# Attention in native float32 with exponentials transposed by TensorE, and half of a weight product beside batch 0

## The chip, the cores and the metric

The kernel runs on one core of a Trainium2 chip. The metric is the device time of one execution in microseconds (us), a median of several runs. Engines are named as the profile names them: PE is TensorE (PEld its weight loads), DVE is VectorE, ACT is ScalarE, POOL is GpSimd, SP is SyncE, which issues the DMAs of this kernel.

## The reference

Four batches, eight heads, 576 positions, head size 64; then two gated products over the 2304 x 512 result. Weights come as float64.

```python
scores = scale * q @ k.T + bias          # scale 1/8, bias -slope[h] * |i - j|
mask = (rel >= 0) & (rel < 128)          # rel = i - j: a causal window of 128
attn = exp(scores - max); attn /= attn.sum(-1) + 1e-9
x = attn @ v                             # to 2304 x 512, heads side by side
x = (x @ w_a) * (x @ w_b) @ w_out        # 512 -> 1536 -> 512
a, b = x @ w1, x @ w2                    # 512 -> 1024
out = (a * b @ w3) @ w_out2              # 1024 -> 1024 -> 512
```

## The kernel before

**Precision.** TensorE takes float32 operands in a reduced form (fp32r), so each float32 value is split in a high and a low part and a product is made of three matmuls: low x high, high x low, high x high. This holds for the scores, for every gated product and for w3 by w_out2.

**Attention.** A unit is one batch and two heads (`units`, 16 of them, batch by batch). Its five query blocks of 128 positions (the last has 64) are done in three runs, `RUNS = ((0, 1), (2, 3), (4,))`. `prep` transposes the unit's q and k on TensorE (ten tiles of 128 x 128) and splits them in a high and a low part. For each run, `scores` makes the three products for each block and head; `step_exps` adds the bias and takes the row's extreme on VectorE (L338), then the exponential and its sum on ScalarE (L344). One run later `norms` makes the reciprocals and `probs` multiplies the exponentials by them, written as two float16 parts (L372, L376, L378), which a DMA transpose issued by SP (L383) turns round. `LAG` runs after the scores, `pv` multiplies by v: v is split in three bfloat16 parts by GpSimd, and five of the part products are made, the two heads in the two halves of the array's columns; v is the stationary operand. `pv_out` splits the result in x_hi and x_lo. `keep_warm` issues matmuls on filler data in the first units. A PSUM pool of three tiles (`ps_t`) holds the transposed q and k and the products with v.

**Beside attention.** `Filler` issues steps of the first group of gated products (group 0: `g1`, L546, and `g2_two`, L572) in tiles of 256 tokens, once the group's six weight tiles are ready and the tokens' attention is finished, worth `FILL` us of TensorE per run. `Stages` works off a list of weight loads and conversions from float64 bits (`convert`: two passes on ScalarE, three on VectorE, one on GpSimd, then the split); `PACE` says how many turns it takes per run, in batch 0 and after it.

**After attention.** The ten steps of group 0 that are left, then groups 1 to 9 of the gated products, tile by tile, all on TensorE at three products each. Beside groups 1 to 4, `w34_parts` makes the product w3 by w_out2, which the last groups use as one weight: two halves of w3's columns, eight row blocks each. A block is four transposes (L454), an eviction and a split, twelve matmuls of 512 columns (L462), an eviction (L464) and a store to DRAM; the two halves are added when they are loaded again.

**Order.** Instructions are ordered by the framework from a simulated schedule, starting from the program's order; each engine then works through its own queue in order.

Of the kernel before, what the change touches and what calls it, by code (L numbers as in the profile page):

```python
# [8 lines left out]
F32 = mybir.dt.float32  # L9
# [25 lines left out]
LAG = 3  # L35
FILL = 2.4
PACE = (0.5, 1.0)
TURN = 400
WARM_UNITS, WARM = 3, 2
# [3 lines left out]
def attention_moe_moe(ctx, tc, q, k, v, w_a, w_b, w_o, w_1, w_2, w_3, w_o2, out):  # L43
# [10 lines left out]
    PSC = 2.0 ** 15  # L54
# [42 lines left out]
    def convert(raw, hi=None, lo=None, use=()):  # L97
# [26 lines left out]

        def s3():
            nc.gpsimd.tensor_tensor(out=ai, in0=ai, in1=es[0], op=ALU.add)  # L126
# [54 lines left out]
    sm_p = asb.enter_context(tc.tile_pool(name="sm_p", bufs=2, side="right"))  # L181
    ps_s = asb.enter_context(tc.tile_pool(name="ps_s", bufs=3, space=PSUM))
# [5 lines left out]
    v_raws = [raw_p.tile([P, NB, P], F32, name=f"v_raw{i}") for i in range(3)]  # L188

    def consts():  # L190
# [30 lines left out]
        for t in [t for ts in raws for t in ts] + v_raws:  # L221
            nc.vector.memset(t[:, NB - 1, :], 0.0)
# [7 lines left out]
    def load_unit(u, which=(0, 1, 2)):  # L230
        b, hp = units[u]
        for x in which:
            s = (q, k, v)[x][b, 2 * hp:2 * hp + 2]
            t = raw_of(u)[x] if x < 2 else v_raws[u % 3]
            for j in range(2):
                nc.sync.dma_start(
                    out=t[:, 0:NB - 1, j * D:(j + 1) * D],
                    in_=s[j, 0:(NB - 1) * P, :].rearrange("(c p) d -> p c d", p=P),
                )
            if x:  # L240
                nc.sync.dma_start(
                    out=t[0:LAST, NB - 1, :].rearrange("p (j d) -> p j d", j=2),
# [4 lines left out]
            for j in range(2):  # L247
                o = slice(j * D, (j + 1) * D)
                nc.sync.dma_start(out=t[o, NB - 1, o], in_=s[j, (NB - 1) * P:S, :])
# [4 lines left out]
    qk, vS = {}, {}  # L254

    def prep(u):


        def part(n):
# [3 lines left out]
            def trans():  # L263
                if n == 0:
                    qk[u] = [tr_p.tile([P, 2 * NB * P], F32R, name=f"qk{x}") for x in "hl"]
# [12 lines left out]
        def v_parts():  # L278

            vr = v_raws[u % 3]  # L280
            r1 = tr_p.tile([P, NB, P], F32, name="v1")
            v2 = tr_p.tile([P, NB, P], BF16, name="v2")
            upper = [t.bitcast(BF16).rearrange("p c (f t) -> p c f t", t=2)[:, :, :, 1] for t in (vr, r1)]
            vS[u] = upper + [v2]
            sub(nc.gpsimd, r1, vr, upper[0])
            sub(nc.gpsimd, v2, r1, upper[1])

        return [part(n) for n in range(len(parts))] + [(v_parts, None)]
# [10 lines left out]
    def scores(run):  # L299
# [4 lines left out]
        for u, i in run:  # L304
            hi, lo = qk[u]
# [23 lines left out]
    def step_exps(u, i):  # L329
# [4 lines left out]
        pe = d["pe"] = sm_p.tile([P, 2, 2 * P], F32, name="pe", bufs=5)  # L334
# [13 lines left out]

    def keep_warm(cnt, x):
# [5 lines left out]
    def norms(run):  # L355
        st = live.pop(run)
        nc.vector.tensor_scalar(
            out=st[:, 2], in0=st[:, 1], scalar1=1.0e-9, scalar2=1.0 / PSC, op0=ALU.add, op1=ALU.mult
        )
        nc.vector.reciprocal(out=st[:, 3], in_=st[:, 2])  # L360

    def probs(u, i):
        m, n, nb, nj = window(i)
        d = live[u, i]
        pe, st = d["pe"], d["st"][:, 3]
        pp = sm_p.tile([P, 2 * 2 * 2 * P], F16, name="pp", bufs=5)[:, 0:2 * nj * n].rearrange(
            "p (a b c) -> p a b c", a=nj, b=2
        )

        for j in range(nj):  # L370
            if i == 0:
                nc.vector.tensor_scalar(  # L372
                    out=pp[:, j, 0, :], in0=pe[:, j, :n], scalar1=st[:, j:j + 1], scalar2=None, op0=ALU.mult
                )
            else:
                nc.scalar.activation(pp[:, j, 0, :], pe[:, j, :n], ACTF.Copy, scale=st[:, j:j + 1])  # L376
        for j in range(nj):
            nc.vector.scalar_tensor_tensor(  # L378
                out=pp[:, j, 1, :], in0=pe[:, j, :n], scalar=st[:, j:j + 1], in1=pp[:, j, 0, :],
                op0=ALU.mult, op1=ALU.subtract,  # L380
            )
        t = sm_p.tile([P, 8 * P], F16, name="pt", bufs=6)[:, 0:2 * nj * n]
        nc.sync.dma_start_transpose(  # L383
            out=t.rearrange("p (g m) -> p g m", m=P), in_=pp.rearrange("p a b c -> p (a b c)")
        )

        order = "p (a b c m) -> p a b c m" if nj == 2 else "p (b c a m) -> p a b c m"
        d["pt"] = t, t.rearrange(order, a=2, b=2, c=nb)
# [4 lines left out]
    def pv(run):  # L393
# [4 lines left out]
        for u, i in run:  # L398
            vs = vS[u]
            m, n, nb, nj = window(i)  # L400
            t, pt = live.pop((u, i))["pt"]
            terms = [
                (max(i - 1, 0) + g, g, hl, z)
                for g in range(nb) for hl, z in ((0, 2), (1, 1), (1, 0), (0, 1), (0, 0))
            ]
            for x, (kb, g, hl, z) in enumerate(terms):
                for j in range(2):
                    c = slice(j * D, (j + 1) * D)
                    nc.tensor.matmul(  # L409
                        ps[c, at:at + m], vs[z][:, kb, c], pt[:, j, hl, g, :],  # L410
                        start=(x == 0), stop=(x == len(terms) - 1),
                    )
            at += m
            if u < WARM_UNITS and m == P:
                keep_warm(WARM, t[:, 0:4 * P])

    def pv_out(run):
# [5 lines left out]
        nc.scalar.activation(x_hi[:, hp, o], ps, ACTF.Copy, scale=1.0 / PSC)  # L423
        nc.vector.scalar_tensor_tensor(
            out=x_lo[:, hp, o], in0=ps, scalar=1.0 / PSC, in1=f32(x_hi[:, hp, o]),
            op0=ALU.mult, op1=ALU.subtract,
        )
# [7 lines left out]
    def mm_tile(n):  # L435
        ps = pools["mm"]
        turn[0] += 1
        return ps[turn[0] % len(ps)].tile([P, n], F32, name="mm")

# [212 lines left out]
    def attention_ops():  # L652

        late = []
        for n in range(NR + LAG):
# [29 lines left out]
            if k == RU - 1 and u + 1 < NU:  # L685
                ops.append(trans[RU][0])
# [27 lines left out]
    pools.update(conv=conv_a, raws=1, cas=2)  # L714
# [11 lines left out]
    for f, g in prep(0):  # L726
        f()
        if g:
            g()
    load_unit(1, (0, 1))  # L730
    side.parts += weight_parts(0)
    fl = Filler()
    warm = sm_p.tile([P, 8 * P], F16, name="pt", bufs=6)[:, 0:2 * P]
    nc.vector.memset(warm, 0.0)
    keep_warm(10, warm)
# [34 lines left out]
    side.parts += w34_parts(late, range(2))  # L770
# [27 lines left out]
```

## Time and profile before

| | |
|---|---|
| median of three runs | 998.87 us (995.44 to 999.41) |
| profiled execution | 995.97 us |
| its span, first to last instruction | 994.2 us |
| TensorE busy | 953.7 us (96%) |
| VectorE busy | 533.0 us (54%) |
| ScalarE busy | 430.4 us (43%) |
| GpSimd busy | 399.5 us (40%) |
| DMA | 85.21 MB, mean 86 GB/s |

The busy shares are means over two stages that differ. A busy TensorE is not one at its peak: matmuls overlap, and each is counted to its modelled end. The price of one among many is read from the distance of starts.

### The profile page before, as it was taken

The page shows a single profiled execution, that of the slowest core. Times are in us where ns is not written, and L with a number is a line of the kernel's source. Part 1 is how long each engine was busy: PE and PEld are TensorE (multiplying, and loading weights), DVE is VectorE, ACT ScalarE, POOL GpSimd, SP SyncE. Part 2 cuts the span into 40 slices and gives each one's busy share as a digit, 9 for nine tenths or more (in the row PEclk, how much of TensorE's full clock was granted, in tenths as well). Part 3 has the DMA queues.
Part 4 walks back from the last instruction along what each step waited for, and adds up shares of the span by engine and source line. Part 5 has one row for each costly group of instructions (what it writes and reads, how often), then busy time and mean ns, then how long its engine had stood idle before and what let it go on. Part 6 is the DMA issues. An engine that isn't in the chain of part 4 may idle for free.

```text
span 994.2 us, 16251 instructions
## 1 busy us (share of the span) xinstructions
PE 953.7 (96%) x6162; PEld 802.6 (81%) x6162; DVE 533.0 (54%) x1188; ACT 430.4 (43%) x1003; POOL 399.5 (40%) x329
## 2 busy tenths in 40 slices
PE   8889898888999999999999999999999999999998
PEld 6558787777988788888888888888888888888886
DVE  5979877775689734566474463442442442422222
ACT  5768867775554434434443342343421321311110
POOL 4344122221688423545362362584741631611111
PEclk9968999998999999999999999999999999999999
DMA  5797786764433222323341240120120120000012
GB/s 131 163 185 154 140 140 134 141 127 85 134 121 106 85 96 84 108 75 106 97 126 59 69 139 22 43 85 1 42 85 1 51 78 1 22 1 1 26 65 101
DMA packets 160079, 85.21 MB, mean 86 GB/s; under 512 B 128001, under 2 KB 148993, under 8 KB 160001
## 3 DMA queue, kind: packets, MB, share of 16 engines
q1 hardware_dynamic: 160000, 84.18, 34.1%
q8 instruction: 48, 0.79, 0.3%
q14 instruction: 31, 0.25, 0.1%
HBM read 58.20 MB, written 8.91 MB: 68 GB/s over the span
## 4 chain that ended last, share of the span: by engine, by line
PE 79%; DMA 7%; DVE 6%; ACT 3%; issue 3%; POOL 1%; SPq 1%; POOLq 0%; ACTq 0%; DVEq 0%
PE mm L546 44%; PE mm L583 11%; PE mm L598 10%; PE mm L462 4%; DMA pt<-pp 4%; PE s L312 3%; PE tr L409 3%; PE tr L269 2%; DVE pp L378 1%; PE mm L572 1%; DVE ca L121 1%; DMA raw<-in_moe_w_a 1%; DVE ca L117 1%; POOL ca L126 1%; PE mm L454 1%
## 5 line engine op out<-in xcount | busy, mean ns | idle before, releaser
L72 POOL TENSOR_TENSOR gl<-g,gh 128x512 fp32r<-128x512 f32 (+1 forms) x108 | 123.9, 1148 | 312.4 <-ACT gh L556 312.1
L553 DVE TENSOR_TENSOR g<-a,mm 128x512 f32<-128x512 f32 (+1 forms) x108 | 64.1, 594 | 212.8 <-PE mm L546 189.8
L126 POOL TENSOR_TENSOR ca<-ca,ce 128x512 int32<-128x512 int32 x76 | 101.3, 1333 | 141.2 <-ACT ce L110 68.6
L556 ACT ACTIVATE gh<-g 128x512 fp32r<-128x512 f32 (+1 forms) x108 | 60.2, 558 | 175.6 <-DVE g L553 175.6
L546 PE MATMUL mm<-x_hi,wlA 128*128 128x512 f32 (+1 forms) x464 | 107.5, 350 | 0.0
L551 ACT ACTIVATE a<-mm 128x512 f32<-128x512 f32 (+1 forms) x108 | 56.0, 519 | 117.5 <-PE mm L546 117.4
L546 PE MATMUL mm<-x_lo,whA 128*128 128x512 f32 (+1 forms) x464 | 104.0, 345 | 0.0
L546 PE MATMUL mm<-x_hi,whA 128*128 128x512 f32 (+1 forms) x464 | 102.9, 343 | 0.0
L546 PE MATMUL mm<-x_hi,wlB 128*128 128x512 f32 (+1 forms) x400 | 99.1, 370 | 2.1 <-DVE g L553 0.8
L546 PE MATMUL mm<-x_lo,whB 128*128 128x512 f32 (+1 forms) x400 | 98.5, 368 | 0.0
L546 PE MATMUL mm<-x_hi,whB 128*128 128x512 f32 (+1 forms) x400 | 98.1, 368 | 0.0
L114 DVE TENSOR_SCALAR ca<-ca 128x512 f32<-128x512 f32 x76 | 46.3, 610 | 91.8 <-ACT ca L107 90.6
L546 PEld LDWEIGHTS mm<-x_lo,whA 128*128 128x128 f32 x464 | 78.1, 192 | 10.5
L546 PEld LDWEIGHTS mm<-x_hi,wlA 128*128 128x128 f32 x464 | 77.7, 192 | 10.8 <-issue 0.4
L546 PEld LDWEIGHTS mm<-x_hi,whA 128*128 128x128 f32 x464 | 77.3, 191 | 10.2
L546 PEld LDWEIGHTS mm<-x_hi,wlB 128*128 128x128 f32 x400 | 70.8, 188 | 15.6 <-ACT a L551 1.3
L107 ACT ACTIVATE ca<-raw 128x512 f32<-128x512 f32 x76 | 50.7, 668 | 72.1 <-DMA raw<-in_moe_w 38.2
L587 DVE TENSOR_TENSOR acc<-acc,mm 128x512 f32<-128x512 f32 (+1 forms) x100 | 61.9, 629 | 36.9 <-PE mm L583 36.6
L546 PEld LDWEIGHTS mm<-x_lo,whB 128*128 128x128 f32 x400 | 71.1, 189 | 12.6
L546 PEld LDWEIGHTS mm<-x_hi,whB 128*128 128x128 f32 x400 | 71.0, 189 | 12.5
L121 DVE SCALAR_TENSOR_TENSOR ca<-raw,ca 128x512 int32<-128x512 int32 x76 | 79.9, 1052 | 1.8
L110 ACT ACTIVATE ce<-raw 128x512 int32<-128x512 uint32 x76 | 50.9, 670 | 60.0 <-POOL ca L126 24.9
(104 smaller groups left out, 1868.7 us busy)
## 6 DMA issues: line engine op xcount, KB each, us to landing
raw<-in_moe_w SPq DMA_DIRECT2D x32, 512.0 KB, 3.7
raw<-in_moe_w_out SPq DMA_DIRECT2D x20, 512.0 KB, 3.6
raw<-in_moe_w_a SPq DMA_DIRECT2D x12, 512.0 KB, 3.6
raw<-in_moe_w_b SPq DMA_DIRECT2D x12, 512.0 KB, 3.6
out<-acc SPq DMA_DIRECT2D x18, 256.0 KB, 2.0
q_raw<-in_q SPq DMA_DIRECT2D x32, 128.0 KB, 2.9
k_raw<-in_k SPq DMA_DIRECT2D x32, 128.0 KB, 2.7
v_raw<-in_v SPq DMA_DIRECT2D x32, 128.0 KB, 2.9
```

The costliest lines, as they stand in the source:

```text
L72: eng.tensor_tensor(out=out, in0=a, in1=b, op=ALU.subtract)
L107: nc.scalar.activation(a, f32(hw), ACTF.Abs)
L110: nc.scalar.activation(e, lw, ACTF.Copy, scale=2.0 ** -29)
L121: nc.vector.scalar_tensor_tensor(out=ai, in0=hw, scalar=-(1 << 30), in1=ai, op0=ALU.bitwise_and, op1=ALU.bitwise_or)
L126: nc.gpsimd.tensor_tensor(out=ai, in0=ai, in1=es[0], op=ALU.add)
L546: nc.tensor.matmul(p, w[:, z, kk, :], x[:, kk, o], start=(y == 0), stop=(y == len(terms) - 1))
L551: nc.scalar.activation(a, ps[0], ACTF.Copy)
L553: nc.vector.tensor_tensor(out=gg, in0=a, in1=ps[1], op=ALU.mult)
L556: nc.scalar.activation(gh, gg, ACTF.Copy)
L583: nc.tensor.matmul(p, w, x, start=(y == 0), stop=(y == len(terms) - 1))
L587: nc.vector.tensor_tensor(out=ya, in0=ya, in1=p, op=ALU.add)
L598: nc.tensor.matmul(p, x, w, start=(y == 0), stop=(y == len(terms) - 1))
```

## The change

Scores: q and k are kept as one float32 tile each, and one native float32 matmul replaces the three products. The exponentials are divided in place on VectorE (in `norms`), transposed by TensorE and moved from PSUM by VectorE or ScalarE; no DMA transpose is left. v is used as loaded, as one native float32 product instead of five. The lag goes from three runs to two. `ps_t` with its three tiles takes the transposed exponentials as well.

The first half of w3 by w_out2 (`EARLY`) moves ahead of group 0's weights: 12 more conversions, eight blocks of four transposes, one eviction and four native float32 matmuls of 512 columns, and a store. The second half stays where it was. `convert` can write its result to a given tile; the conversion pools grow from one raw tile and two converted ones to two and three; `PACE` changes; `keep_warm` is issued in the first unit alone.

```diff
-LAG = 3
+LAG = 2
+PES, PTS = 6, 6
-PACE = (0.5, 1.0)
+PACE = (1.8, 0.5)
+EARLY = (0,)
-WARM_UNITS, WARM = 3, 2
+WARM_UNITS, WARM = 1, 2
...
             def parted():
-                hi, lo = qk[u]
-                nc.scalar.activation(hi[:, o], hold[0], ACTF.Copy)
-                nc.vector.tensor_tensor(out=lo[:, o], in0=hold[0], in1=f32(hi[:, o]), op=ALU.subtract)
+                evict(nc.scalar if n == 1 else nc.vector, qk[u][:, o], hold[0])
...
-            for x, (a, b) in enumerate(((lo, hi), (hi, lo), (hi, hi))):
-                for j in range(nj):
-                    r = slice(j * D, (j + 1) * D) if nj == 2 else slice(0, P)
-                    nc.tensor.matmul(
-                        ps[j][:, at:at + n], a[r, qs], b[r, ks], start=(x == 0), stop=(x == 2)
-                    )
+            for j in range(nj):
+                r = slice(j * D, (j + 1) * D) if nj == 2 else slice(0, P)
+                nc.tensor.matmul(ps[j][:, at:at + n], t[r, qs], t[r, ks], start=True, stop=True)
...
+        for u, i in run:
+            m, n, nb, nj = window(i)
+            d = live[u, i]
+            for j in range(nj):
+                pe = d["pe"][:, j, :n]
+                nc.vector.tensor_scalar(
+                    out=pe, in0=pe, scalar1=d["st"][:, 3, j:j + 1], scalar2=None, op0=ALU.mult
+                )
...
+        pe = d.pop("pe")
+        ps = ps_t.tile([P, W], F32, name="tr")[:, 0:nj * n]
         for j in range(nj):
...
+            for g in range(nb):
+                o = (j * nb + g) * P
+                nc.tensor.transpose(ps[:, o:o + P], pe[:, j, g * P:(g + 1) * P], ident)
+        t = d["pt"] = sm_p.tile([P, W], F32, name="pt", bufs=PTS)[:, 0:nj * n]
+        evict(nc.vector if i in (0, NB - 1) else nc.scalar, t, ps)
...
+            for g in range(nb):
                 for j in range(2):
                     c = slice(j * D, (j + 1) * D)
+                    q0 = (j * nb + g) * P if nj == 2 else g * P + j * LAST
                     nc.tensor.matmul(
-                        ps[c, at:at + m], vs[z][:, kb, c], pt[:, j, hl, g, :],
-                        start=(x == 0), stop=(x == len(terms) - 1),
+                        ps[c, at:at + m], v_raws[u % 3][:, max(i - 1, 0) + g, c], t[:, q0:q0 + m],
+                        start=(g == 0), stop=(g == nb - 1),
                     )
...
+    def w34_plain(pool, halves):
...
+            def trans(a):
+                t.append(pool.tile([P, NJ, P], F32, name="w3t", bufs=2))
+                ps = mm_tile(W).rearrange("p (j f) -> p j f", j=NJ)
+                for j in range(NJ):
+                    nc.tensor.transpose(ps[:, j, :], a[:, j * P:(j + 1) * P], ident)
+                nc.scalar.activation(t[0], ps, ACTF.Copy)
+
+            def gemm(a):
+                ps = mm_tile(DM)
+                for j in range(NJ):
+                    nc.tensor.matmul(ps, t[0][:, j, :], o[0][:, j, :], start=(j == 0), stop=(j == NJ - 1))
+                sb = pool.tile([P, DM], F32, name="w34s", bufs=1)
+                nc.vector.tensor_copy(out=sb, in_=ps)
+                nc.sync.dma_start(out=w34[half, f * P:(f + 1) * P, :], in_=sb)
...
-    pools.update(conv=conv_a, raws=1, cas=2)
+    pools.update(conv=conv_a, raws=2, cas=3)
...
-    side.parts += weight_parts(0)
+    side.parts += w34_plain(w34_p, EARLY) + weight_parts(0)
...
-    side.parts += w34_parts(late, range(2))
+    side.parts += w34_parts(late, [h for h in range(2) if h not in EARLY])
```

## Rows read from the trace of the kernel before

**Rows 1.** Busy time of each engine by stage, granted clock, DMA share.
```profile
core 0: us, PE busy (x) PEld busy (x) DVE busy (x) ACT busy (x) POOL busy (x), PEclk, DMA share, GB/s
...
50.00:100.00 50.00, 45.77 (x475) 36.06 (x476) 43.94 (x148) 37.84 (x113) 22.47 (x19) 0.76 0.90 171
100.00:150.00 50.00, 44.98 (x615) 39.43 (x614) 38.77 (x145) 36.61 (x118) 11.81 (x12) 1.00 0.82 139
...
275.00:600.00 325.00, 323.54 (x1596) 273.05 (x1597) 195.88 (x280) 139.19 (x244) 163.16 (x125) 1.00 0.31 96
```

**Rows 2.** The chain that ended last: shares of the span by engine.
```profile
PE 79%; DMA 7%; DVE 6%; ACT 3%; issue 3%; POOL 1%; SPq 1%; POOLq 0%; ACTq 0%; DVEq 0%
```

**Rows 3.** TensorE in order of time, end of attention (start, duration, instruction).
```profile
249.63 0.20 PE L409 MATMUL tr<-pt,v_raw 128*64 128x64 f16 x2
```

**Rows 4.** The score line: ns least/median/most, first and last start; whole, then 0:65.
```profile
L312 PE MATMUL s<-qkh,qkl x144: 275/362/775, 7.7 to 231.5; 64*128 64x256 f32 x96, 64*128 64x128 f32 x32, 128*128 128x256 f32 x16
...
L312 PE MATMUL s<-qkh,qkl x40: 275/412/775, 7.7 to 63.7; 64*128 64x256 f32 x26, 64*128 64x128 f32 x10, 128*128 128x256 f32 x4
```

**Rows 5.** DMA issues up to 250 us: count, KB each, us to landing.
```profile
raw<-in_moe_w_a SPq DMA_DIRECT2D x3, 512.0 KB, 4.6
pt<-pp SPq DMA_TRANSPOSE x80, 3.2
```

**Rows 6.** SP's queue in order of time, in batch 2.
```profile
148.22 1.24 SPq L383 DMA_TRANSPOSE pt<-pp  x1
149.50 1.12 SPq L236 DMA_DIRECT2D q_raw<-in_q  x2
```

**Rows 7.** TensorE in order of time, beside group 3, with one block of w3.
```profile
560.96 0.60 PE L454 MATMUL mm<-ident,ca 128*128 128x128 f32 x4
561.31 1.18 PE L546 MATMUL mm<-x_hi,wlA 128*128 128x512 f32 x4
...
567.79 1.07 PE L462 MATMUL mm<-oh,w3l 128*128 128x512 f32 x4
...
570.51 0.62 PE L583 MATMUL mm<-gh,wlA 128*128 128x512 f32 x2
```

**Rows 8.** TensorE in order of time, in batch 1.
```profile
117.98 0.28 PE L409 MATMUL tr<-pt,v 128*64 128x128 f16 x4
...
118.26 0.28 PE L409 MATMUL tr<-pt,v 128*64 128x128 f16 x4
...
121.25 0.49 PE L269 MATMUL tr<-ident,k_raw 128*128 128x128 f32 x3
121.67 0.33 PE L312 MATMUL s<-qkl,qkh 64*128 64x128 f32 x2
...
122.12 0.27 PE L312 MATMUL s<-qkl,qkh 64*128 64x256 f32 x2
122.23 0.28 PE L312 MATMUL s<-qkh 64*128 64x256 f32 x2
```

**Rows 9.** VectorE by line and form up to 250 us: busy us, mean ns, idle before.
```profile
L378 DVE SCALAR_TENSOR_TENSOR pp<-pe,st,pp 128x256 f16<-128x256 f32 x112 | 61.5, 586 | 6.4 <-ACT pp L376 6.2
L338 DVE CUSTOM_DVE_ANT_0 pe<-s,relb 128x256 f32<-128x256 f32 x112 | 43.7, 418 | 12.8 <-PE s L312 12.6
...
L372 DVE TENSOR_SCALAR pp<-pe,st 128x128 f16<-128x128 f32 x32 | 8.1, 291 | 2.2 <-DMA pt<-pp 2.0
...
L121 DVE SCALAR_TENSOR_TENSOR ca<-raw,ca 128x512 int32<-128x512 int32 x6 | 4.1, 684 | 0.0
...
L114 DVE TENSOR_SCALAR ca<-ca 128x512 f32<-128x512 f32 x6 | 2.5, 423 | 2.0 <-POOL wlA L72 1.0 <-ACT ca L107 1.0
```

**Rows 10.** ScalarE by line and form up to 250 us.
```profile
L344 ACT ACTIVATE pe<-pe,st 128x256 f32<-128x256 f32 x112 | 55.6, 499 | 6.0 <-DVE st L338 5.9
L376 ACT ACTIVATE pp<-pe,st 128x256 f16<-128x256 f32 x112 | 49.4, 500 | 8.8 <-DMA pt<-pp 6.1 <-ACT pe L344 0.9 <-DVE st L360 0.8
...
L107 ACT ACTIVATE ca<-raw 128x512 f32<-128x512 f32 x6 | 4.0, 666 | 1.4 <-DMA raw<-in_moe_w_a 0.7 <-DMA raw<-in_moe_w_out 0.7
```

More of the change, by code (lines that the diff above doesn't have):

```diff
@@ L95, in load_rows, with convert @@
         return raw
-    def convert(raw, hi=None, lo=None, use=()):
+    def convert(raw, hi=None, lo=None, use=(), into=None):
         hw, lw = raw[:, :, 1], raw[:, :, 0].bitcast(U32)
@@ L125, in s3 @@
         def s3():
-            nc.gpsimd.tensor_tensor(out=ai, in0=ai, in1=es[0], op=ALU.add)
+            to = ai if into is None else into.bitcast(I32)
+            nc.gpsimd.tensor_tensor(out=to, in0=ai, in1=es[0], op=ALU.add)
         if hi is None:
@@ L181, in attention_moe_moe @@
     sm_p = asb.enter_context(tc.tile_pool(name="sm_p", bufs=2, side="right"))
+    w34_p = asb.enter_context(tc.tile_pool(name="w34a", bufs=1, side="right"))
     ps_s = asb.enter_context(tc.tile_pool(name="ps_s", bufs=3, space=PSUM))
@@ L188, in attention_moe_moe @@
     v_raws = [raw_p.tile([P, NB, P], F32, name=f"v_raw{i}") for i in range(3)]
+    warm = raw_p.tile([P, W], F16, name="warm")
     def consts():
@@ L241, in load_unit @@
                 nc.sync.dma_start(
-                    out=t[0:LAST, NB - 1, :].rearrange("p (j d) -> p j d", j=2),
+                    out=t[0:LAST, NB - 1],
                     in_=s[:, (NB - 1) * P:S, :].rearrange("j p d -> p j d"),
@@ L248, in load_unit, with evict @@
                 o = slice(j * D, (j + 1) * D)
-                nc.sync.dma_start(out=t[o, NB - 1, o], in_=s[j, (NB - 1) * P:S, :])
+                nc.sync.dma_start(out=t[o, NB - 1, j], in_=s[j, (NB - 1) * P:S, :])
     cols = [(x, i, (x * NB + i) * P) for x in range(2) for i in range(NB)]
     parts = [cols[0:3], cols[3:7], cols[7:10]]
-    qk, vS = {}, {}
+    qk = {}
+    def evict(eng, out, in_):
+        if eng is nc.scalar:
+            eng.activation(out, in_, ACTF.Copy)
+        else:
+            eng.tensor_copy(out=out, in_=in_)
     def prep(u):
@@ L264, in trans @@
                 if n == 0:
-                    qk[u] = [tr_p.tile([P, 2 * NB * P], F32R, name=f"qk{x}") for x in "hl"]
+                    qk[u] = tr_p.tile([P, 2 * NB * P], F32, name="qk")
                 ps = ps_t.tile([P, W], F32, name="tr")[:, 0:o.stop - o.start]
@@ L271, in parted @@
             def parted():
-                hi, lo = qk[u]
-                nc.scalar.activation(hi[:, o], hold[0], ACTF.Copy)
-                nc.vector.tensor_tensor(out=lo[:, o], in0=hold[0], in1=f32(hi[:, o]), op=ALU.subtract)
+                evict(nc.scalar if n == 1 else nc.vector, qk[u][:, o], hold[0])
             return trans, parted
[L278 to L288, printed above, removed]
+        return [part(n) for n in range(len(parts))]
     live = {}
@@ L304, in scores @@
         for u, i in run:
-            hi, lo = qk[u]
+            t = qk[u]
             m, n, nb, nj = window(i)
@@ L333, in step_exps @@
         ps = d.pop("ps")
-        pe = d["pe"] = sm_p.tile([P, 2, 2 * P], F32, name="pe", bufs=5)
+        pe = d["pe"] = sm_p.tile([P, 2, 2 * P], F32, name="pe", bufs=PES)
         st = d["st"]
@@ L347, in step_exps, with norms @@
             )
+    def norms(run):
+        st = live.pop(run)
+        nc.vector.tensor_scalar(out=st[:, 2], in0=st[:, 1], scalar1=1.0e-9, scalar2=None, op0=ALU.add)
+        nc.vector.reciprocal(out=st[:, 3], in_=st[:, 2])
+        for u, i in run:
[6 more added lines that the diff above has]
+                )
     def keep_warm(cnt, x):
@@ L353, in keep_warm @@
             nc.tensor.matmul(ps[:, :x.shape[1]], x[:, 0:P], x, start=(y == 0), stop=(y == cnt - 1))
[L355 to L360, printed above, removed]
     def probs(u, i):
@@ L414, in pv @@
             if u < WARM_UNITS and m == P:
-                keep_warm(WARM, t[:, 0:4 * P])
+                keep_warm(WARM, warm)
     def pv_out(run):
@@ L422, in pv_out @@
         ps = outs.pop(run)[:, :m]
[L423 to L427, printed above, removed]
+        nc.scalar.activation(x_hi[:, hp, o], ps, ACTF.Copy)
+        sub(nc.vector, x_lo[:, hp, o], ps, f32(x_hi[:, hp, o]))
         if hp == NP - 1:
@@ L438, in mm_tile, with product, load @@
         return ps[turn[0] % len(ps)].tile([P, n], F32, name="mm")
+    def w34_plain(pool, halves):
+        NJ = W // P
+        parts = []
+        def product(half, f, o):
+            t = []
+            def trans(a):
[11 more added lines that the diff above has]
+                nc.sync.dma_start(out=w34[half, f * P:(f + 1) * P, :], in_=sb)
+            return trans, gemm
+        for half in halves:
+            o = []
+            def load(j, half=half, o=o):
+                if j == 0:
+                    o.append(pool.tile([P, NJ, DM], F32, name="o32", bufs=1))
+                return load_rows(w_o2, half * NJ + j, 0)
+            for j in range(NJ):
+                parts.append((
+                    lambda j=j, load=load: load(j),
+                    lambda raw, j=j, o=o: convert(raw, into=o[0][:, j, :]),
+                ))
+            for f in range(FB):
+                parts.append((
+                    lambda f=f, half=half: load_rows(w_3, f, half),
+                    lambda raw, f=f, half=half, o=o: convert(raw, use=product(half, f, o)),
+                ))
+        return parts
     def w34_parts(pool, halves):
@@ L727, in attention_moe_moe @@
         f()
-        if g:
-            g()
+        g()
     load_unit(1, (0, 1))
-    side.parts += weight_parts(0)
+    side.parts += w34_plain(w34_p, EARLY) + weight_parts(0)
     fl = Filler()
-    warm = sm_p.tile([P, 8 * P], F16, name="pt", bufs=6)[:, 0:2 * P]
     nc.vector.memset(warm, 0.0)
-    keep_warm(10, warm)
+    keep_warm(10, warm[:, 0:2 * P])
     paid = 0.0
```

38 lines of the change are left out of this document (4 added, 34 removed).

## Prediction, made before the result was known

> **What bounds the kernel now.** I read the busy times by stage first [rows 1]. From 275 us on, TensorE is busy for 323.5 of 325 us at a granted clock of 1.00: nothing but its own instructions sets the time there, and an instruction taken out of that stretch is worth its full length. Before that the picture is another one. From 50 to 150 us VectorE is busy 83 of 100 us, TensorE 91 (a figure that holds the drain of every matmul), the DMA engines 0.82 to 0.90, and the granted clock is 0.76 in the first half. The chain that ended last [rows 2] agrees: TensorE has 79% of it, and what lies outside is mostly DMA (7%) and VectorE (6%), which is attention. So the span of 994.2 us is cut in two: attention up to 249.8 us, where the last product with v is issued [rows 3], and 744.4 us in which TensorE alone decides.
>
> The reader is to see in attention that no engine is full and several are nearly so. The first scores start at 7.7 us and those of the last unit at 231.5 us, so 16 units take 14.0 us each [rows 4]. For each unit SP issues five DMA transposes of 1.25 us and ten loads of 0.56 us, 11.9 of 14.0 us [rows 6], and a transpose lands 3.2 us after its issue [rows 5]. In the first 65 us the median score matmul lasts 412 ns against a least one of 275, which is how the lower clock looks [rows 4]. Durations are of the profiled execution: 994.2 us span, 1.8 us around it, 995.97 us in all. The median of the three runs shown is 998.87, 2.9 above it; I make the sum in the profiled execution and add 2.9 at the end.
>
> **What leaves the late stretch.** For half of w3 by w_out2, eight blocks each lose 12 matmuls and four transposes. Twelve take 2.72 us (567.79 to 570.51) and four transposes 0.35 us (560.96 to 561.31) [rows 7]: 8 x 3.07 = 24.6 us, all on the path. The other engines' part of these blocks goes too and is worth nothing there, since TensorE covers it.
>
> **TensorE in attention, per unit.** Before: one block of keys costs the v product ten matmuls, 0.28 us (117.98 to 118.26), five products of which each runs the two heads side by side [rows 8]. A unit has seven such blocks and two of half the columns: 2.2 us, or 0.44 for one product. Two heads' scores of 256 columns take 0.11 us side by side (122.12 to 122.23) [rows 8]; alone each would take half of 0.227 us, the price of 512 columns [rows 7]. One product of a unit's scores (three such pairs, one single of 256 columns, a pair of 128 at about the same 0.11) is then some 0.57 us side by side and 0.91 one after the other. Transposes go from ten to 26 a unit, as 16 of the exponentials are added.
>
> A native float32 matmul is not in this trace. Its bounds are one product and five, which is what the v product spends now; the scores spend three. Both operands split in two halves make four partial products, between the three and the five of the rows, so I take four, an estimate. The second unknown is whether the two heads still run side by side. Product with v: 1.8 us if they do, 3.5 if not. Scores: 2.3 or 3.65. I take the middle, 2.65 and 3.0, because the rows show overlap of single-pass forms only. A transpose is 0.088 us in the late stretch [rows 7] and 0.14 in attention, where a weight switch is in it (121.25 to 121.67 for three) [rows 8]: 26 make 2.3 to 3.6, I take 2.7. Sum 8.4 us, from 6.4 to 10.8, where before it was 2.2 + about 2.3 + 1.2 = 5.7.
>
> The Trainium skill, "FP8 and Floating Point Precision", section TensorE Precision Notes, says true FP32 takes four passes through the array. No run here shows it yet; by it the sum above stands as it is, and the product moved forward gets a third dearer than the three it replaces.
>
> **Fill-in work.** Followed through the code turn by turn, group 0's weights are complete at run 18 instead of 16, and in both versions 14 gate steps of 24 matmuls and 12 output steps of 12 are issued within attention, ten items left behind. At 0.113 us for 256 columns [rows 7] that is 54 us, with switches some 57, or 4.8 per unit of batches 1 to 3. So TensorE has 13.2 us a unit there (11.2 to 15.6).
>
> **VectorE and ScalarE per unit.** Gone are nine second-half subtractions (586 ns for 256 columns) and three of q and k [rows 9]; taken over are nine divisions, two evictions of q and k and two of transposed exponentials. By starts rather than durations (a running group overlaps its neighbours) I count 10.2 us now and 8.7 after: score step 2.9, sums 0.9, division 2.5, evictions 1.6, x_lo 0.8. A division of 256 columns isn't in the rows; 128 columns take 291 ns and a two-operand pass over 256 takes 418 [rows 9], I take 300, and all nine between those bounds move a unit by under 1.2 us. ScalarE falls by about 2.2 us: seven scalings a unit of 500 ns and two evictions of q and k go, three evictions of transposed exponentials come; the exponentials, 499 ns each for 256 columns, stay [rows 10], and with them some 6.9 us. GpSimd loses two splits of v. All of these lie under 13.2, so they cost nothing while TensorE is the longer; without that cover VectorE would set 9.1.
>
> **Batch 0.** It takes in 18 conversions instead of six in the time of four units, with 1.8 turns a run. VectorE: 4 x 8.7 + 18 x 1.7 (three passes of 423 to 684 ns [rows 9]) + 8 copies of 0.6 = 70 us. TensorE: 4 x 8.4, 32 native matmuls of 4 x 0.227 (29 us), transposes 2.8, warm-up about 4: 69 us. VectorE's share when it was fullest was 0.88 [rows 1]: 70 / 0.88 = 80 us, against 56 now. Conversions themselves are not the limit: load 4.6 us [rows 5], ScalarE two passes of 0.67 [rows 10], VectorE 1.7, on two buffers, 3.8 each, 68 in all. The new loads and the eight stores go through SP's queue, which has lost 6.2 us of transposes a unit: hidden.
>
> **New waits.** TensorE now transposes the exponentials, and behind that instruction stand the product with v, fill-in work and the next scores. It waits for VectorE's divisions, which stand behind the next run's score step, and three PSUM buffers now serve four tiles a run instead of two. LAG of two runs, 8 us, against a chain of 6 to 7 us covers it; I put it at nothing, and price it below.
>
> **The sum.** Start 7.7, batch 0 80, twelve units of 13.2 (158.4), tail 8 instead of 18 because the DMA is out of it and LAG is shorter: 254.1 us, 4.3 later than 249.8. With 24.6 saved: 994.2 + 4.3 - 24.6 = 973.9, 975.7 with what lies around, 978.6 as a median: 2% less.
>
> **Rivals.** (a) The heads of native matmuls do run side by side: 6.4 + 4.8 = 11.2 a unit, TensorE still longest. Twelve units save 24 us, so 955. For it: both forms overlap now [rows 8]. Chance 0.22. (b) They don't, and each pays its passes in full: 15.6 a unit is +29, batch 0's TensorE goes to 79 / 0.88 = 90, +10: 1017, slower. For it: nothing in the rows shows a float32 pass of several products overlapping. It decides from about 15 us a unit. Chance 0.18. (c) The PSUM buffers: a transposed tile waits for ScalarE, which has four exponentials of 0.5 us [rows 10] ahead of it. A wait of 0.7 us in each of 36 runs is 25 us: 1004; below 0.4 us a run the kernel is still faster. Chance 0.08. (d) The change doesn't give its main effect, as batch 0 takes up what the late stretch saves: with one conversion in flight at 5.5 us instead of 3.8, batch 0 is 99 us, +19: 998, no change. For it: raw tiles are freed by VectorE, the fullest engine there. Chance 0.10. The forecast, with a pace between 12.0 and 14.4 us a unit 964 to 993, has 0.42.
>
> A clock that stays low in batch 0 would belong to (d): its 34 us of attention matmuls at twice the length add up to that. [...]
>
> **Numbers.** A measurement here can tell about 0.5%, 5 us. Faster than 993.9: nearly all of the forecast and (a), 0.63. Within 5 us: (d) and an edge, 0.12. Slower: (b), (c) and the far edge of (d), 0.25. The range takes in (a) with a quicker batch 0 and reaches to most of (b): 948 to 1015.
>
> **What would show it.** In the changed profile: blocks of w3 by w_out2 after attention eight instead of 16, 24.6 us less; native scores and v products at 0.9 us for 512 columns, or by spacing half of that where heads overlap; the end of attention at 254 us, batch 0's at about 88; the granted clock near 1.00. It is wrong if the pace of batches 1 to 3 isn't TensorE's 13 us a unit, or if batch 0 lasts beyond 100 us.

## The result

The changed kernel takes 988.37 us (986.99 to 988.91), the kernel before beside it 998.14: a ratio of 0.9904 [0.988, 0.9927]. The forecast was 978.6, so the sign was right and the gain less than half of the 2% foreseen. The profiled execution spans 986.6 us, where the sum gave 973.9: 12.7 us are to be found.

The changed kernel's busy time by stage (as in [rows 1]), from two answers:

```profile
core 0: us, PE busy (x) PEld busy (x) DVE busy (x) ACT busy (x) POOL busy (x), PEclk, DMA share, GB/s
0.00:50.00 50.00, 34.83 (x238) 24.66 (x238) 35.17 (x145) 27.93 (x86) 13.52 (x21) 0.89 0.69 171
50.00:100.00 50.00, 44.99 (x236) 26.69 (x236) 38.65 (x119) 31.64 (x81) 11.52 (x10) 0.91 0.52 155
100.00:150.00 50.00, 49.46 (x387) 38.51 (x386) 40.63 (x131) 32.69 (x94) 16.79 (x15) 1.00 0.38 101
...
300.00:600.00 300.00, 299.03 (x1467) 252.27 (x1466) 166.74 (x231) 113.20 (x200) 139.42 (x108) 1.00 0.23 76
```

TensorE is full from 100 us on, and the DMA share has fallen from 0.90 and 0.82 [rows 1] to 0.52 and 0.38. VectorE has 0.70 and 0.77 of the first two stretches. The 0.88 on which the batch 0 term stood is reached only for a while, as between 30 and 60 us (26.56 of 30 us, 0.89), where TensorE is busy for only 18.72 us:

```profile
30.00:60.00 30.00, 18.72 (x146) 13.51 (x146) 26.56 (x86) 18.46 (x52) 7.33 (x6) 0.83 0.61 167
```

In the chain that ended last TensorE's share has risen from 79% to 83%, and DMA's fallen from 7% to 4% [rows 2]:

```profile
PE 83%; DVE 6%; DMA 4%; ACT 3%; issue 2%; POOL 1%; SPq 0%; DVEq 0%; ACTq 0%; POOLq 0%
```

Where the 12.7 us are is read from the last v product of a unit (64 columns, as in [rows 3]), in order of time on TensorE; here those of units 4, 6 and 16 of the changed kernel:

```profile
93.45 0.45 PE L390 MATMUL tr<-pt,v_raw 128*64 128x64 f32 x8
...
132.67 0.45 PE L390 MATMUL tr<-pt,v_raw 128*64 128x64 f32 x8
...
266.50 0.45 PE L390 MATMUL tr<-pt,v_raw 128*64 128x64 f32 x8
```

Attention ends at 266.9, not 254.1, and what follows takes 986.6 - 266.9 = 719.7 us against 744.4 before, 24.7 less where the forecast had 24.6. So the whole miss lies in attention. In the forecast's terms unit 4 is at 7.7 + 80 + 8 = 95.7; it came at 93.5. The last ten units took 133.8 us, 13.4 each (forecast 13.2). The two between, units 5 and 6, took 39.2 us instead of 26.4: 12.8 too many.

What stood in them is the early half. The product's line (ns least/median/most, first and last start), and VectorE's last pass of single conversions in order of time:

```profile
L436 PE MATMUL mm<-o,w3t x64: 592/592/1061, 62.4 to 111.7; 128*128 128x512 f32 x64
```

```profile
60.02 0.68 DVE L122 SCALAR_TENSOR_TENSOR ca<-raw,ca 128x512 int32<-128x512 int32 x1
...
90.51 0.69 DVE L122 SCALAR_TENSOR_TENSOR ca<-raw,ca 128x512 int32<-128x512 int32 x1
...
102.84 0.68 DVE L122 SCALAR_TENSOR_TENSOR ca<-raw,ca 128x512 int32<-128x512 int32 x1
...
118.98 0.69 DVE L122 SCALAR_TENSOR_TENSOR ca<-raw,ca 128x512 int32<-128x512 int32 x1
```

There are eight from 60.02 to 102.84, one every 42.8 / 7 = 6.1 us: near the 5.5 of rival (d), not the 3.8 that the forecast used. When unit 4 is done, five of eight blocks are multiplied and 12 of 18 conversions made; the last one is at 119.0. Three blocks and group 0's weights fell into units 5 and 6; three blocks alone are 11.6 us of TensorE at the price read below.

The price of a native matmul, on float32 operands taken whole, can now be read. One early block, eight records for four matmuls, then the next block's transposes; and the v product of two heads, eight native matmuls of 128 columns, before scores:

```profile
69.50 3.60 PE L436 MATMUL mm<-o,w3t 128*128 128x512 f32 x8
72.94 0.60 PE L430 MATMUL mm<-ident,ca 128*128 128x128 f32 x4
73.37 0.60 PE L371 MATMUL tr<-ident,pe 128*128 128x128 f32 x4
...
171.25 1.09 PE L390 MATMUL tr<-pt,v_raw 128*64 128x128 f32 x16
172.27 1.13 PE L309 MATMUL s<-qk 64*128 64x256 f32 x8
```

By the distance of starts, four of 512 columns take 3.44 us, 0.86 each: 3.8 times the 0.227 of one product [rows 7], where four were taken; a block's four transposes take 0.43. The Trainium skill, "FP8 and Floating Point Precision", TensorE Precision Notes, states four passes, and this trace agrees. At that price eight of 128 columns, one after the other, would take 1.7 us; the eight of the v product, two heads in the two halves of the array's columns, take 1.02. The native matmuls added in run g2 (section 6) are as long but fill the whole array, and eight of them last 1.95 us from first start to last end, where the v product's eight last 1.09:

```profile
57.10 1.95 PE L771 MATMUL mm<-ident 128*128 128x128 f32 x16
```

So the heads do run side by side, the mechanism of rival (a). By spacing a unit then costs 2.2 us of v product, 2.4 of scores and 2.7 of transposes, 7.3 where 8.4 was taken.

### The profile page after: what moved, and what is told of

Its sections match the earlier page's. It is cut to its first block, busy times and chain, and to the rows that moved or that the text cites. A ratio compares the mean times of both kernels' runs of the same rounds, so it can differ in the third digit from the quotient of the medians.

```text
span 986.6 us, 14240 instructions
## 1 busy us (share of the span) xinstructions
PE 954.7 (97%) x5362; PEld 787.7 (80%) x5362; DVE 510.3 (52%) x1172; ACT 391.2 (40%) x895; POOL 350.5 (36%) x293
## 4 chain that ended last, share of the span: by engine, by line
PE 83%; DVE 6%; DMA 4%; ACT 3%; issue 2%; POOL 1%; SPq 0%; DVEq 0%; ACTq 0%; POOLq 0%
PE mm L569 45%; PE mm L606 11%; PE mm L621 10%; PE s L309 3%; PE tr L371 3%; PE tr L390 3%; PE mm L485 2%; PE mm L436 2%; PE mm L595 2%; PE tr L279 2%; DVE ca L122 1%; DMA raw<-in_moe_w_a 1%; DVE ca L115 1%; DMA raw<-in_moe_w 1%; ACT pe L339 1%
## 5 line engine op out<-in xcount | busy, mean ns | idle before, releaser
L128 POOL TENSOR_TENSOR ca<-ca,ce 128x512 int32<-128x512 int32 x72 | 95.3, 1324 | 135.2 <-ACT ce L111 54.1
L339 ACT ACTIVATE pe<-pe,st 128x256 f32<-128x256 f32 (+1 forms) x144 | 68.2, 475 | 36.7 <-DVE st L333 36.6
L569 PEld LDWEIGHTS mm<-x_lo,whB 128*128 128x128 f32 x400 | 71.1, 189 | 12.6
L122 DVE SCALAR_TENSOR_TENSOR ca<-raw,ca 128x512 int32<-128x512 int32 x76 | 77.8, 1023 | 1.6
```

The source lines that it names most:

```text
L122: nc.vector.scalar_tensor_tensor(out=ai, in0=hw, scalar=-(1 << 30), in1=ai, op0=ALU.bitwise_and, op1=ALU.bitwise_or)
L128: nc.gpsimd.tensor_tensor(out=to, in0=ai, in1=es[0], op=ALU.add)
L339: nc.scalar.activation(pe[:, j, :n], pe[:, j, :n], ACTF.Exp, bias=st[:, 0, j:j + 1], scale=-1.0, accum_out=st[:, 1, j:j + 1],)
L569: nc.tensor.matmul(p, w[:, z, kk, :], x[:, kk, o], start=(y == 0), stop=(y == len(terms) - 1))
```

## The experiments

Ratios are to the kernel before on the same chip; "e1" names the version with both halves late, from which several others start. "Attention ends" is the start of the last unit's v product plus 0.4 us.

**1. Both halves late (e1).**

```diff
-EARLY = (0,)
+EARLY = ()
```


> Both halves of w3 by w_out2 stay after attention; the native float32 attention alone is kept. Theory A (the early half's TensorE work, 8 blocks of about 3.9 us, stands on the path between 62 and 112 us, since its first product comes only after a start in which TensorE is starved): attention ends some 28 to 34 us earlier and the late stretch is 24.6 us longer, so 978 to 985 us, no slower than the changed kernel at 988. Rival B (the early half is hidden beside batch 0, as the prediction had it, and attention by itself is too slow): attention ends at most 12 us earlier, so 1000 us or more.

981.12 us, 0.9851 [0.9827, 0.9875]. Attention ends at 235.0:

```profile
234.58 0.45 PE L390 MATMUL tr<-pt,v_raw 128*64 128x64 f32 x8
```

So native attention alone is worth 14.9 us of attention (249.8 before), and the early half costs 31.9 us there to save 24.7 later. It is a loss of 7 us by the medians, 5 by the ratios. In total next to nothing of it is hidden: its own TensorE work is 32 x 0.86 + 8 x 0.43 = 31 us.

**2. What of the early half costs: three cuts.** One of four native matmuls in each block kept (e2); its conversions cut to ScalarE's first pass (e3); both (k3).

```diff
-                for j in range(NJ):
-                    nc.tensor.matmul(ps, t[0][:, j, :], o[0][:, j, :], start=(j == 0), stop=(j == NJ - 1))
+                for j in range(1):
+                    nc.tensor.matmul(ps, t[0][:, j, :], o[0][:, j, :], start=(j == 0), stop=(j == 0))
```


> Of the four native matmuls of each early block only the first is made (24 of 32 left out, 0.86 us each by the trace, 20.6 us; the output lacks those products). Loads, conversions, transposes, evictions and stores stay. Theory A: TensorE is the limit in that stretch, so 17 to 21 us less, 967 to 971 us. Rival C (the 18 conversions on ScalarE and VectorE set the pace of batch 0, TensorE has room): at most 5 us less, 983 us or more.

```diff
-                    lambda raw, j=j, o=o: convert(raw, into=o[0][:, j, :]),
+                    lambda raw, j=j, o=o: one_pass(raw, into=o[0][:, j, :]),
...
-                    lambda raw, f=f, half=half, o=o: convert(raw, use=product(half, f, o)),
+                    lambda raw, f=f, half=half, o=o: one_pass(raw, use=product(half, f, o)),
```


> The 12 early conversions are cut to their first ScalarE pass (one ScalarE, three VectorE and one GpSimd pass left out of each, so the early product is of other values); loads, products and stores stay. Theory A: the products stay on the path and only their start moves forward, 5 to 12 us less, 976 to 983 us. Rival C (conversions set the pace): VectorE alone loses 12 x 1.7 = 20 us, so 17 us or more less, 971 us or below.

> The changed kernel with both cuts together: the early product takes one of its four native matmuls a block, 24 of 32 left out, and the twelve conversions of the early half are cut to ScalarE's first pass, so that half of w3 by w_out2 is not the reference's. Each cut alone ended attention 10.0 and 8.7 us sooner. Theory N (the early half's price is the sum of what it costs TensorE and what its conversions cost the others): 17 to 20 us, attention ends at 247 to 250, device 967 to 970. Rival O (both cuts free the same wait): 9 to 13 us, device 975 or above.

e2: 977.54, 0.9817 [0.9794, 0.984], attention 10.0 us sooner than in the changed kernel, half of the 20.6 taken out and between the two theories. e3: 979.56, 0.9838 [0.9814, 0.9862], 8.7 sooner, as theory A had it. k3: 966.15, 0.9684 [0.9664, 0.9705], 22.6 sooner, more than the sum of the two and than theory N's 20. The price is thus products and conversions together. With one cut alone, the engine of the other fills up between 50 and 100 us: VectorE is busy 0.96 in e2 (0.77 in the changed kernel), TensorE 0.97 in e3 (0.90 in the changed kernel; 48.74 of 50 us). From e2:

```profile
50.00:100.00 50.00, 40.45 (x269) 25.65 (x269) 47.77 (x146) 38.18 (x101) 14.00 (x11) 0.88 0.62 177
```

**3. The weights first, then the early half (e4).**

```diff
-    side.parts += w34_plain(w34_p, EARLY) + weight_parts(0)
+    side.parts += weight_parts(0) + w34_plain(w34_p, EARLY)
```


> Group 0's weights are loaded before the early half instead of after it; the work is the same. The early half then runs at half a turn per run beside batches 1 to 3, where TensorE is full. Theory A: no room there either, and TensorE's starved start stays, so 986 to 1000 us. Rival D (what costs is only that 12 conversions crowd the first 60 us and put off group 0): 10 us less or better, 978 us or below.

1002.51, 1.0068 [1.0041, 1.0094]; attention ends at 283.2, the products run from 92.5 to 163.4. This is worse than both theories: attention is 48.2 us longer than in e1, 17 more than the early half's own work on TensorE. In batches 1 to 3, where TensorE sets the pace, nothing of the products is hidden; and from 50 to 100 us, before most of them, VectorE is busy 46.99 of 50 us and TensorE only 36.04 (44.76 in e1), so the conversions held attention up as well.

**4. Is TensorE the pace of batches 1 to 3?** On e1, each score made twice from batch 1 on.

```diff
-                nc.tensor.matmul(ps[j][:, at:at + n], t[r, qs], t[r, ks], start=True, stop=True)
+                for y in range(2 if u >= NP else 1):
+                    nc.tensor.matmul(ps[j][:, at:at + n], t[r, qs], t[r, ks], start=True, stop=True)
```


> The kernel with both halves late, and in batches 1 to 3 each native score matmul is issued twice (the same result). That is some 2.4 us more of TensorE per unit by the spacing in the changed kernel's trace (0.85 + 1.6 us for a unit's three runs), 29 us in 12 units. Theory A (TensorE sets the pace of batches 1 to 3): 22 to 30 us more than 981, so 1003 to 1011 us. Rival E (VectorE, ScalarE or the waits between them set it): at most 10 us more, 991 us or less.

1010.07, 1.0142 [1.0126, 1.0158]: 29 us added by the estimate from spacing, 29 paid. TensorE is the pace there, as forecast.

**5. Scores by three products again (f3), on e1.**

```diff
-            for j in range(nj):
...
+            for x, (a, b) in enumerate(((lo, hi), (hi, lo), (hi, hi))):
+                for j in range(nj):
...
+                        ps[j][:, at:at + n], a[r, qs], b[r, ks], start=(x == 0), stop=(x == 2)
```


> The kernel with both halves late, and the scores as before the change: q and k split in a high and a low part (two more ScalarE evictions a unit, VectorE subtracts instead of copying) and three products. By the spacing in the traces three products side by side are 1.7 to 2.3 us a unit against about 2.4 native. Theory A: TensorE gets 0.1 to 0.7 us a unit back, 0 to 11 us less, 970 to 981 us. Rival E (ScalarE's 0.75 and VectorE's 0.3 us more a unit count): 6 to 15 us more, 987 us or above.

1005.02, 1.0086 [1.0056, 1.0115]. Native scores are worth 24 us; theory A had the sign wrong, and rival E had at most 15. The stages of f3 show part of it; the granted clock is the last but two of the columns:

```profile
50.00:100.00 50.00, 44.56 (x349) 36.63 (x349) 34.31 (x133) 30.05 (x92) 7.42 (x7) 0.80 0.24 54
100.00:150.00 50.00, 45.57 (x381) 36.64 (x380) 33.28 (x146) 30.65 (x99) 1.48 (x2) 0.86 0.24 54
```

and those of e1:

```profile
50.00:100.00 50.00, 44.76 (x366) 37.03 (x365) 34.27 (x130) 30.16 (x93) 10.11 (x10) 0.89 0.27 66
100.00:150.00 50.00, 48.82 (x451) 40.38 (x452) 36.08 (x164) 32.71 (x110) 2.20 (x3) 1.00 0.33 74
```

The clock is 0.80 and 0.86 instead of 0.89 and 1.00, 0.09 and 0.14 of 50 us each: up to 12 of the 24 us, an estimate from these rows. Why it is lower, and what the splitting of q and k costs beside it, was not taken apart.

**6. Room on TensorE in batch 0.** 27 us of native matmuls on the identity, ready at any time, added in eight runs of batch 0, to the kernel before (g1) and to e1 (g2).

```diff
+        if 4 <= n < 12:
+            ps = mm_tile(W)
+            for y in range(16):
+                o = slice(y % 4 * P, (y % 4 + 1) * P)
+                nc.tensor.matmul(ps[:, o], ident, ident, start=True, stop=True)
```


> The kernel before, and in each of eight runs of batch 0 sixteen more native float32 matmuls of 128 columns on the identity tile (0.213 us each by the trace, 27 us in all, no loads, no conversions, no result used). Theory A': with the old attention TensorE has room in batch 0, since it waits there for DMA transposes and VectorE, so at most 15 us more, 1011 us or less against 996. Rival G: a low clock and the order in TensorE's queue make it pay in full or more, 23 us or more, 1019 us or above.

> The kernel with both halves late, and in each of eight runs of batch 0 sixteen native float32 matmuls of 128 columns on the identity tile (27 us of TensorE, ready at any time, no loads or conversions, result unused). The early half itself cost 32 us of attention. Theory A'' (there is room on TensorE in batch 0, but the early half's products come too late to use it, after their conversions): at most 16 us more, 997 us or less. Rival J (no room in batch 0 at all): 24 us or more, 1005 us or above.

g1: 1010.71, 1.014 [1.0122, 1.0157]: 14 of 27 us paid. g2: 994.5, 0.9969 [0.9948, 0.9991]: 0.0118 above e1, 12 of 27. Ready work is half hidden, and the early half was not. It differs from this work in two ways, in being late and in bringing conversions with it, and these runs don't separate the two. In g2 the clock has a part in it as well. From 50 to 100 us the granted clock is 1.00 in g2, 0.89 in e1:

```profile
50.00:100.00 50.00, 47.52 (x420) 41.48 (x418) 30.70 (x124) 26.45 (x84) 5.36 (x6) 1.00 0.22 49
```

From 0 to 50 us it is 0.97 against 0.84. By 0.13 and 0.11 of 50 us the clock can give back up to 12 us, an estimate, so g2 doesn't show how much of the half was room. In g1 the clock over these 100 us hardly moves (0.80 and 0.94, before 0.97 and 0.76), so there the hidden half is room.

**7. Other covers for batch 0 that gave nothing.** On e1: conversions spread thinner (f4, `PACE = (0.9, 0.5)`), batch 0's divisions on ScalarE (h1), more filler matmuls (h2, `WARM_UNITS, WARM = 4, 4`, 64 in all), a longer lag (k2, `LAG = 3`). On the changed kernel: the divisions on ScalarE (h3).

```diff
+                if u < NP:
+                    nc.scalar.activation(pe, pe, ACTF.Copy, scale=d["st"][:, 3, j:j + 1])
+                    continue
```


> The kernel with both halves late, and half as many conversion turns a run in batch 0 (0.9 instead of 1.8), so that group 0's six conversions are spread over batch 0. Theory A (batch 0 is held by VectorE and by a low clock of a starved TensorE): the same six conversions anyway, 975 to 982 us. Rival F (their crowding in the first 40 us is what makes batch 0 slow): 10 us less or better, 971 us or below.

> The kernel with both halves late, and in batch 0 alone the divisions are made by ScalarE (36 of them, about 0.42 us each by the starts of the old scalings) instead of VectorE. In its trace five divisions take 1.3 us while GpSimd is idle and 3.4 us while GpSimd works on a weight; they hold 16% of the chain in batch 0. Theory H (batch 0 is long because VectorE's divisions are stretched beside GpSimd's conversions): 5 to 12 us less than 981, 969 to 976 us. Rival I (batch 0 is held by the low clock of TensorE or by ScalarE): within 3 us, 978 to 984 us, or slower by ScalarE's 15 us.

> The kernel with both halves late and four filler matmuls of 512 columns after each block of all four units of batch 0 (64 instead of 8; 12 us more of TensorE at the higher level). Its clock in the first 82 us is 0.83. Rival I (the low clock makes batch 0 long): the clock rises above 0.93 and the time falls by 4 to 10 us, 971 to 977 us. Theory H (VectorE holds batch 0): no gain, 980 to 992 us.

> Both halves of the product late, and the product with v three runs behind its scores instead of two; nothing else. Theory M (batch 0 is held by TensorE's wait for divided and transposed exponentials, which a longer lag covers): 3 to 8 us less than the 981.1 us with a lag of two. Rival L (the chain of a run is covered by two runs already): within 2 us, 979 to 983.

> The changed kernel as it is, early half and all, with the divisions of batch 0 on ScalarE as in the run with both halves late. Theory H: VectorE's stretched divisions delay the early half's conversions too, 6 to 15 us less than 988, 973 to 982 us. Rival I: within 3 us of 988 or slower.

f4: 981.64, 0.9853 [0.9825, 0.988]. h1: 981.97, 0.9841 [0.981, 0.9872]. h2: 987.81, 0.9901 [0.9874, 0.9928]. k2: 981.2, 0.9836 [0.9816, 0.9856]. h3: 988.75, 0.9914 [0.9886, 0.9942]. None gains on its base. The expectation of h2 asked for a clock above 0.93, but from 0 to 82 us it rose only from 0.83 to 0.90; what a full clock is worth there stays open. In h1 ScalarE is what fills up; 30 to 60 us of h1:

```profile
30.00:60.00 30.00, 20.91 (x133) 15.79 (x133) 20.08 (x68) 29.13 (x86) 14.84 (x12) 0.67 0.55 140
```

and of e1, where VectorE is at 0.95:

```profile
30.00:60.00 30.00, 22.29 (x134) 15.82 (x135) 28.39 (x82) 20.70 (x56) 12.54 (x10) 0.62 0.53 137
```

**8. What a conversion costs.** On e1, the six conversions of group 0's weights cut to the first pass and the split (k1, by `one_pass` as in 2).

> Both halves of the product late again, and the six conversions of group 0's weights, which run beside batch 0, cut to ScalarE's first pass and the split, so that the weights of that group are not the reference's. Without the early half attention ended at 234.9 us and the device time was 981.1. Theory K (conversions that run beside batch 0 hold it up by their passes on GpSimd and VectorE, as eight to twelve us of the twelve conversions of the early half did): 8 to 12 us less, attention ends at 223 to 227, device 969 to 973. Rival L (six conversions are too few, batch 0 is held by its start and by waits from engine to engine): at most 4 us less, device 977 or above.

968.1, 0.9709 [0.9689, 0.9728]; attention ends 12.6 us sooner: 2.1 us a conversion, for three passes on VectorE (1.7 in the forecast's sum), one on ScalarE and one on GpSimd, a little more than theory K had. The granted clock from 50 to 100 us is 1.00 here, 0.89 in e1. How VectorE pays is seen in e1's trace. GpSimd and then VectorE in order of time, 46 to 52 us:

```profile
45.73 1.38 POOL L128 TENSOR_TENSOR ca<-ca,ce 128x512 int32<-128x512 int32 x1 [4.22 <-DVE ca L122]
47.94 1.26 POOL L128 TENSOR_TENSOR ca<-ca,ce 128x512 int32<-128x512 int32 x1 [0.83 <-DVE st L347]
49.16 1.31 POOL L73 TENSOR_TENSOR wlA<-ca,whA 128x512 fp32r<-128x512 f32 x1
```

and:

```profile
45.91 1.29 DVE L346 TENSOR_SCALAR st<-st 128x4 f32<-128x4 f32 x2
...
47.98 3.44 DVE L353 TENSOR_SCALAR pe<-pe,st 128x256 f32<-128x256 f32 x5
```

Two passes over four elements last 1.29 us, until 47.2, and GpSimd's pass ends at 47.1; five divisions last 3.44 us beside two more. So GpSimd's two passes of a conversion were given to VectorE, in the changed kernel (p1) and in e1 (p2):

```diff
-            nc.gpsimd.tensor_tensor(out=to, in0=ai, in1=es[0], op=ALU.add)
+            side_eng().tensor_tensor(out=to, in0=ai, in1=es[0], op=ALU.add)
...
-        sub(nc.gpsimd, lo, f, f32(hi))
+        sub(side_eng(), lo, f, f32(hi))
+
+    def side_eng():
+        return nc.vector if pools.get("run", 99) < 18 else nc.gpsimd
```


> The changed kernel with GpSimd's two passes of a conversion (the integer sum and the subtraction of the split) given to VectorE in the first 18 runs of attention, some 22 passes of about 1.3 us each on GpSimd; low bits of those operands can differ, since VectorE forms the integer sum in another precision. In the changed kernel five divisions took 3.4 us beside two such passes and 1.3 us without. Theory P (VectorE stands still while a pass of GpSimd holds what both need, and that lengthens attention): although VectorE gets 22 passes of some 0.65 us more, 4 to 12 us less, device 976 to 984. Rival Q (it is VectorE's own work that counts): 22 x 0.65 = 14 us of VectorE, half of it or more on the path, 7 to 14 more, device 995 or above.

> Both halves of the product late, and the same passes of the six conversions of group 0's weights given to VectorE, twelve passes; low bits of those operands can differ. Theory P: 3 to 8 us less than the 981.1 us without this edit, device 973 to 978. Rival Q: 12 x 0.65 = 8 us of VectorE, 4 to 8 more, device 985 or above.

p1: 981.06, 0.9838 [0.9824, 0.9853]: 7 us less than the changed kernel, as theory P had it, though VectorE has more to do. Two things are in this gain, less VectorE's added work: a division takes 347 ns on average up to 100 us instead of 420, and the conversions come quicker, one every 5.5 us instead of 6.1 for the same eight, with the integer sum at 0.68 us on VectorE where GpSimd took 1.27. No run takes the two apart. p2: 979.7, 0.9816 [0.98, 0.9833]: 1.4 less than e1 by the medians, 3.5 by the ratios, at or below the low end of theory P and on the other side of e1 from Q; the two intervals overlap a little, and attention ends 1.8 us sooner. By line in p2, up to 100 us:

```profile
L356 DVE TENSOR_SCALAR pe<-pe,st 128x256 f32<-128x256 f32 x42 | 12.6, 347 | 0.2
...
L122 DVE SCALAR_TENSOR_TENSOR ca<-raw,ca 128x512 int32<-128x512 int32 x6 | 4.1, 686 | 0.0
```

and in e1:

```profile
L353 DVE TENSOR_SCALAR pe<-pe,st 128x256 f32<-128x256 f32 x41 | 16.8, 462 | 0.1
...
L122 DVE SCALAR_TENSOR_TENSOR ca<-raw,ca 128x512 int32<-128x512 int32 x6 | 6.1, 1019 | 0.0
```

The early half alone, on the kernel before, was not tried.

## Why the prediction was right or wrong

- **Late stretch, right.** 24.7 us against 24.6.
- **A unit's TensorE, right in kind, 1.1 us too high.** 7.3 against 8.4, since the heads do run side by side. That TensorE sets the pace there is shown by f2. A unit still takes 13.4 us in the changed kernel, because the fill-in starts only at 112.6 us, when most of group 0's weights are made: it is 13.4 - 7.3 = 6.1 a unit over ten units, not 4.8 over twelve. That 13.4 is so near the 13.2 is luck, as two errors offset each other. In e1 the twelve units of batches 1 to 3 take 153 us, 12.75 each.
- **Batch 0, the step that failed.** "It takes in 18 conversions instead of six in the time of four units", and those units in 80 us. The 80 us came out (93.5 for 95.7), but by luck: they were worked out for 18 conversions and eight blocks, and 12 and five were done in them. A conversion came every 6.1 us, where the sum had 3.8, so that six conversions and three blocks stood in units 5 and 6 and made them 12.8 us longer. This is rival (d), whose 5.5 came without a working, on top of a part of (a). The step that failed is thus the cover: that 18 conversions and the products behind them fit into four units and so cost attention no more than a batch 0 of 80 us. In its place e1 shows that the early half costs attention 31.9 us. The 0.88 share of VectorE came from 50 to 100 us of the kernel before, of which the last 17 us are batch 1 already. The "56 now" was four times the mean pace; with the forecast's start and tail it puts unit 4's last v product at 7.7 + 56 + 18 = 81.7, and the trace of before has it at 83.3:

```profile
83.34 0.25 PE L409 MATMUL tr<-pt,v 128*64 128x64 f16 x4
```

- **The tail of 8, too short.** The last scores start at 251.9, the last v product at 266.5, 14.6 us later. In batch 0 the distance is wider still: unit 4's last scores are made by 56.2, in the row below, and its last v product starts 37 us later (29 before). So the 80 and the 8 hold as a sum up to the v product, and not each by itself; two runs of 4 us are not what lies between scores and v product there:

```profile
53.23 2.97 PE L309 MATMUL s<-qk 64*128 64x256 f32 x10
```

- **TensorE's 69 us beside VectorE's 70 in the same 80 us, wrong.** Of the early half's 31 us on TensorE none is hidden in total (e1 against the changed kernel: 31.9 us). Ready matmuls are hidden by half (g1). That the product's place behind its conversions loses the rest fits e2, e3 and k3, but is not shown by itself.
- **VectorE's passes, mis-sized for a reason that was not in the sum.** A division took 420 ns up to 100 us, 355 from 150 to 250 us, instead of 300, and VectorE can stand still beside GpSimd (taking GpSimd's passes off batch 0 is worth 7 us net, by p1).
- **The clock, named under (d), low as feared.** In e1 it is 0.84 from 0 to 50 us, 0.89 from 50 to 100, and 0.62 between 30 and 60, where TensorE is busy for 22.29 of 30 us; more filler (h2) raised this to 0.74 and lost 5 us by the ratios all the same. In the changed kernel it is 0.89 and 0.91, no lower than in e1, so by these rows it is not what makes the early half dear.
- **New waits at nothing, right for batches 1 to 3.** There TensorE is full, so rival (c) did not come, nor (b); and a lag of three runs changes nothing in e1 (k2).
- **What stays open** is how k1's 12.6 us divide between VectorE's passes and the clock, which rose with them, and how p1's 7 us divide between VectorE's standstill and quicker conversions.

The best version is not the changed kernel: with both halves late and no GpSimd beside batch 0 (p2) it is 0.9816, with both halves late alone 0.9851. Their intervals overlap a little, so the order of these two is not sure.

## What to carry to other kernels

Work that is moved under another stage has to be ready when the engine has room: count by the trace when each piece can start (here one conversion per 6.1 us), not only whether the busy times add up to less than the stage. A product of three fast matmuls, moved as one native one, became a quarter dearer here (31 us for 24.7), so more than a fifth of it has to be hidden before it gains at all. A start-up stage is read by itself, with its own first and last rows, not by a window that reaches into the next stage.

## What the runs showed of the hardware

A pass on GpSimd can stop VectorE, and not in proportion: two VectorE passes over four elements ended 0.1 us after a 1.38 us pass of GpSimd. Of the six last VectorE passes of conversions in e1 four took 0.68 to 0.69 us, as in p2, and two that began within 0.5 us of the start of a GpSimd pass took 1.74 and 1.64, which makes the mean of 1019 ns. VectorE's pass that reads scores from PSUM keeps its 418 ns, with GpSimd (e1, 417) or without (p2). The Trainium skill, "SBUF — State Buffer", Terms and "Who interferes with whom", states that VectorE and GpSimd share a pair of ports that one of them holds for a whole instruction; these rows agree. What the standstill alone costs here no run shows; taking GpSimd off batch 0 is worth 7 us net (p1).

Native float32 matmuls whose weights fill half of the array's columns run side by side like those of the kernel before: eight of 128 columns in 1.02 us, where one after the other they would take 1.7 at the price of the full array.
